# The float32 value products of the first attention batch: 64 columns of the array against 128

## The chip, the cores and the metric

The kernel runs on one core of a Trainium2 chip. The metric is the device time of one execution in microseconds (us); before the change it is 1199.45 us, the median of three runs from 1198.36 to 1200.13. Five engines work side by side, each through its own instructions in order: TensorE (PE, with its weight loads PEld), VectorE (DVE), ScalarE (ACT), GpSimd (POOL) and SyncE (SP), which here issues the DMA transfers.

## The reference

Four batches of eight heads, 576 positions, head width 64. In each head only the scores within `tau` of the row's largest one take part in the softmax. Behind the attention stand two feed-forward layers, all in float32:

```python
scores = scale * np.matmul(q, k.transpose(0, 1, 3, 2))
thresh = np.max(scores, axis=-1, keepdims=True) - tau
scores = np.where(scores >= thresh, scores, -1000000000.0)
scores = scores - np.max(scores, axis=-1, keepdims=True)
attn = np.exp(scores)
attn = attn / (np.sum(attn, axis=-1, keepdims=True) + 1e-09)
return np.matmul(attn, v).astype(np.float32)
...
return (silu * val @ w_out).astype(np.float32)      # width 512 -> 1536 -> 512
...
return (h * h @ w_out).astype(np.float32)           # width 512 -> 2048 -> 512
```

## The kernel before

**Tiles of attention.** Heads are handled in pairs, an even and an odd one; a batch has four pairs and a pair nine tiles of 128 rows of scores, so a batch is 36 tiles. For each tile TensorE forms the scores (`QK`, L575, 128x288 twice over), VectorE takes the row's maximum (`RED`, L587), ScalarE the exponential and the threshold (`EXP`, L593 and L595), VectorE masks and sums (`MASK`, L604) and takes the reciprocal (L610), GpSimd divides (`NORM`, L615), and TensorE transposes the tile in five 128x128 pieces (`TR`, L635). Scores have two buffers: the scores of a tile wait until the mask of the tile two before has been taken.

**The products with the values.** Four times in a pair (`AV`, parts 1, 4, 6, 8 of the nine tiles) five chunks of values are multiplied with the transposed tiles and summed in one PSUM bank. In the later batches this is done on numbers split into a rounded and a remaining part, with 128 columns of values (L694). In the first batch (`whole` is true there) it is done in float32 at once (L691): the five chunks lie beside each other in `vf`, 64 columns each, in a part of the tile `x2` that is not needed yet (`flat`). An even head's result goes to the lower 64 partitions of the bank and an odd head's to the upper 64 (`mr`); ScalarE copies that half to `xF`. The values come by DMA (`whole_values`, L452). The transposed tiles of the first batch lie in `ptf`, in the same `x2`, copied out by ScalarE and in one tile of nine in part by VectorE (L48, L50). One such product is in the program one instruction; on the engine it is two weight loads and two matmuls.

**Work around it.** A loader brings the weights of the first layer in 30 pieces of 256 columns: a DMA (L121), an absolute value on ScalarE (L130), four steps on VectorE (L132, L134, L138, L140), a rounding copy on ScalarE (L48) and a subtraction on GpSimd (L56). Its steps are spread over the tile loop by `loader.start` and `loader.tick`. From the end of the first batch on, feed-forward work on finished rows fills TensorE between the tiles (L219, L264); attention is over at about 460 us, and the rest is the two layers (L219, L264, L310).

**What sets the order.** The loop over tiles calls these functions in a fixed sequence with offsets of priority (`early0`, `early`), and a scheduler then orders each engine's instructions by priorities and its own costs. So another cost of one instruction can move others. The lines that matter here:

```python
c0 = 5 * 640 + h % 4 * VW
hd["vf"] = flat[:, c0 : c0 + VW].rearrange("p (c d) -> p c d", d=D)
...
mm(o[mr, :n], hd["vf"][:, SLOT[k], :], ptf[:, k, lo : lo + n], start=(k == 0), stop=(k == 4))
```

Of the kernel before, what the change touches and what calls it, by code (L numbers as in the profile page):

```python
# [18 lines left out]
P = 128  # L19
B, H, S, D = 4, 8, 576, 64  # L20
# [13 lines left out]
VW = 5 * D  # L34
# [28 lines left out]
def attention_moe(tc, qkv, qk0, tau, w1, w2, out, cfg):  # L63
    nc = tc.nc
    ops = Ops(nc)
    mm = nc.tensor.matmul
# [316 lines left out]
    for j in range(LIVE):  # L383
        c0 = LAST + j * PIECE
# [53 lines left out]
    flat = x2[0][1].rearrange("p c t -> p (c t)")  # L438
    ptf = flat[:, : 5 * 640].rearrange("p (s q) -> p s q", q=640)

    def whole(p, i):

        ways = cfg["way"][p // NPAIR % len(cfg["way"])]
        return p < NPAIR and ways[i] in "FEKD"

    def whole_values(h):
        hd = heads[h]
        if any(whole(h // 2, i) for i, x in PARTS.items() if x[2] == hd["odd"]):
            c0 = 5 * 640 + h % 4 * VW
            hd["vf"] = flat[:, c0 : c0 + VW].rearrange("p (c d) -> p c d", d=D)  # L450
            a = 2 * S + hd["odd"] * VW
            nc.sync.dma_start(flat[:, c0 : c0 + VW], qkv[h // 2, :, a : a + VW])  # L452

    def values(hd, h, raw):
        odd = hd["odd"]
        whole_values(h)
        if all(whole(h // 2, i) for i, x in PARTS.items() if x[2] == odd):
            return
        v = raw[:, 2 * S + odd * VW : 2 * S + (odd + 1) * VW].rearrange("p (c d) -> p c d", d=D)
        vs = hd["vs"] = qp.tile([P, 5, P], F32R, name=f"vs{h}", tag="vs", bufs=3)  # L460
        hi, lo = vs[:, :, odd * D : (odd + 1) * D], vs[:, :, (1 - odd) * D : (2 - odd) * D]
        ops.copy(cfg["vh"], hi, v)
        ops.sub(cfg["vl"], lo, v, hi.bitcast(F32))
# [84 lines left out]
    SLOT = (0, 1, 4, 2, 3)  # L548
# [132 lines left out]
    def AV(t):  # L681
        b, p, i = tiles[t]
        lo, n, odd, segs = PARTS[i]
        hd = heads[b * H + 2 * p + odd]
        no, o = mp1.tile()
        mr = slice(D, P) if odd else slice(0, D)
        cr = slice(0, D) if odd else slice(D, P)
        one = whole(b * NPAIR + p, i)
        if one:
            for k in range(5):  # L690
                mm(o[mr, :n], hd["vf"][:, SLOT[k], :], ptf[:, k, lo : lo + n], start=(k == 0), stop=(k == 4))  # L691
        else:
            for k in range(10):
                mm(o[:, :n], hd["vs"][:, SLOT[k % 5], :], pt[:, k, lo : lo + n], start=(k == 0), stop=(k == 9))  # L694
        base = b * S
        out_x = [(xF[mr, p, base + dst : base + dst + w], slice(src, src + w)) for dst, src, w in segs]

        def main():
            for x_, sl in out_x:
                ops.copy("A" if not one else cfg["om"], x_, o[mr, sl])  # L700
            if one:
                end()

        def fin():
            for x_, sl in out_x:
                nc.vector.tensor_tensor(x_, x_, o[cr, sl], op=ALU.add)
            end()

        def end():
            if i == 8 and p == NPAIR - 1:  # L710
                fstate["done"] = b

        if one:
            mp1.post(no, (cfg["om"], main))
        else:
            mp1.post(no, ("A", main), ("D", fin))
# [58 lines left out]
    def work(i):  # L775

        fstate["credit"] += cfg["rate"]
        if avq:
            at_(AV, avq.pop(0))
            if fstate["credit"] < cfg["extra"]:  # L780
                return
        if fstate["credit"] > 0:
            y = at_(fill_group)
            if y is None:
                fstate["credit"] = 0
            else:
                fstate["credit"] -= y
# [19 lines left out]
    for i in range(NTILE + lag + 1):  # L807
# [36 lines left out]
        if i < NTILE:  # L844
            b, p, k = tiles[i]
# [184 lines left out]
def program(arrays):  # L1030
    import concourse.bacc as bacc

    nc = bacc.Bacc("TRN2", target_bir_lowering=False, num_devices=1, dynamic_dma_scratch_size=1024)
    args = [nc.dram_tensor(n, a.shape, mybir.dt.from_np(a.dtype), kind="ExternalInput").ap() for n, a in arrays]
    out = nc.dram_tensor("out_0_dram", (NT, DM), F32, kind="ExternalOutput").ap()
    with tile.TileContext(nc) as tc:
        attention_moe(tc, *args, out, CFG)
    return nc
# [9 lines left out]
```

## Time and profile before

| what | value |
|---|---|
| median of three runs | 1199.45 us |
| the profiled execution, its own time | 1198.72 us |
| its span in the trace | 1196.9 us |
| PE / DVE / ACT / POOL busy over the span | 97% / 73% / 54% / 25% |
| first batch's products with the values (L691) | 160 matmuls, 20.3 to 117.5 us |

The times of the trace count from the start of the span; 1.8 us of the execution lie outside it. The shares over the whole span are a mean over stages that differ: attention alone to about 118 us, attention with feed-forward work between to about 460, and feed-forward layers after that. A busy PE is one on which a matmul is under way; matmuls overlap, so durations of single matmuls add up to more than the time they take, and the distance from one start to the next is what a matmul costs. "issue" is waiting for nothing that the profile shows.

### The profile page before, as it was taken

The numbers are of one execution on the slowest core, as the hardware profiler recorded it, in microseconds if no ns is written. First come the engines' busy times: TensorE is split into PE (matmuls) and PEld (weight loads), VectorE is DVE, ScalarE is ACT, GpSimd is POOL, SyncE is SP. The second block draws the span as 40 slices with busy tenths as digits, with TensorE's granted clock in tenths as the row PEclk, the third lists the DMA queues.
The fourth block names the chain that finished last, engine by engine and source line by source line (L and its number), as shares of the span: only waits on it lengthen the run. The fifth ranks groups of instructions, "written<-read, shape, count | busy, mean of one in ns | idle before, by whom it ended". The sixth has DMA issues, their size and how long they took to land.

```text
span 1196.9 us, 20191 instructions
## 1 busy us (share of the span) xinstructions
PE 1162.6 (97%) x7008; PEld 1074.8 (90%) x7008; DVE 868.2 (73%) x2143; ACT 652.1 (54%) x1622; POOL 293.8 (25%) x417
## 2 busy tenths in 40 slices
PE   5999998999999999999999999999999999999998
PEld 4555887999999999999999999999999899999997
DVE  6877997799989895789965954468449748754443
ACT  5777887888777774545432532145546425533221
POOL 4445875676776663000000000000000000000000
PEclk9999998999999999999999999999999999999999
DMA  5664452444334310332310300003002201100111
GB/s 177 151 182 127 127 134 66 109 116 110 94 97 106 93 36 1 108 104 80 98 36 7 108 29 1 1 18 104 21 1 80 62 1 54 36 1 1 53 54 53
DMA packets 40853, 84.79 MB, mean 71 GB/s; under 512 B 5936, under 2 KB 6960, under 8 KB 40752
## 3 DMA queue, kind: packets, MB, share of 16 engines
q1 hardware_dynamic: 40752, 83.52, 24.9%
q8 instruction: 55, 0.90, 0.3%
q14 instruction: 46, 0.38, 0.1%
HBM read 52.23 MB, written 4.72 MB: 48 GB/s over the span
## 4 chain that ended last, share of the span: by engine, by line
PE 79%; DVE 9%; DMA 3%; ACT 3%; issue 2%; POOL 2%; SPq 1%; POOLq 0%; DVEq 0%; ACTq 0%
PE mm L219 30%; PE mm L310 15%; PE mm L264 9%; PE s L575 5%; PE bank L635 5%; PE bank L219 4%; PE bank L264 4%; PE bank L694 4%; PE bank L691 3%; DMA wr<-in_w_dram 2%; DVE e L604 2%; DVE nm L587 1%; POOL e L615 1%; DMA raw<-in_qkv_dram 1%; DVE xs_k L56 1%
## 5 line engine op out<-in xcount | busy, mean ns | idle before, releaser
L219 PE MATMUL mm<-xs_k,w 128*128 128x384 f32 (+1 forms) x2400 | 413.2, 330 | 0.5 <-ACT x L48 0.5
L219 PEld LDWEIGHTS mm<-xs_k,w 128*128 128x128 f32 x2400 | 407.8, 188 | 2.5 <-ACT x L48 0.7
L310 PE MATMUL mm<-w,k_u 128*128 128x512 f32 x864 | 201.3, 391 | 0.3 <-DVE k_u L56 0.3
L310 PEld LDWEIGHTS mm<-w,k_u 128*128 128x128 f32 x864 | 161.5, 188 | 34.0 <-DVE k_u L56 1.0
L635 PE MATMUL bank<-ident,e 128*128 128x128 f32 x720 | 162.9, 278 | 6.4 <-POOL e L615 1.9
L219 PE MATMUL bank<-xs_m,w 128*128 128x288 f32 x720 | 137.1, 325 | 2.4 <-DVE xs_m L56 1.7
L615 POOL TENSOR_SCALAR e<-e,r 128x576 f32<-128x576 f32 x144 | 113.8, 791 | 83.6 <-DVE r L610 34.4
L604 DVE SCALAR_TENSOR_TENSOR e<-s,thr,e 128x577 f32<-128x577 f32 x144 | 117.0, 813 | 14.7 <-ACT thr L595 7.2
L48 ACT ACTIVATE k_u<-k_th 128x384 fp32r<-128x384 f32 (+1 forms) x148 | 76.3, 516 | 90.0 <-DVE k_th L294 47.0
L587 DVE TENSOR_REDUCE nm<-s 128x1 f32<-128x576 f32 x144 | 108.3, 753 | 17.7 <-PE s L575 16.6
L635 PEld LDWEIGHTS bank<-ident,e 128*128 128x128 f32 x720 | 95.2, 141 | 28.7 <-issue 15.9
L56 DVE TENSOR_TENSOR k_u<-k_th,k_u 128x384 fp32r<-128x384 f32 (+1 forms) x148 | 81.2, 549 | 47.8 <-ACT k_u L48 47.4
L219 PEld LDWEIGHTS bank<-xs_m,w 128*128 128x128 f32 x720 | 111.1, 189 | 5.1 <-DVE xs_m L56 3.4
L593 ACT ACTIVATE e<-s,nm 128x576 f32<-128x576 f32 x144 | 107.4, 746 | 14.3 <-PE bank L635 7.0
L655 ACT ACTIVATE pt<-bank 128x384 fp32r<-128x384 f32 (+1 forms) x216 | 92.1, 437 | 35.1 <-PE bank L635 28.9
L293 ACT ACTIVATE k_th<-mm 128x384 f32<-128x384 f32 x96 | 46.3, 483 | 111.0 <-PE mm L219 110.9
L264 PE MATMUL mm<-k_u,w 128*128 128x384 f32 (+1 forms) x624 | 106.1, 327 | 0.6 <-DVE k_u L56 0.4
L264 PEld LDWEIGHTS mm<-k_u,w 128*128 128x128 f32 x624 | 103.7, 188 | 1.0 <-DVE k_u L56 0.6
L694 PE MATMUL bank<-pt,vs 128*128 128x256 f32 (+1 forms) x480 | 93.5, 324 | 1.3 <-POOL pt L56 1.2
L575 PE MATMUL s<-kh,qs 128*128 128x288 f32 x256 | 78.1, 319 | 14.2 <-DVE qs L484 7.2
L294 DVE TENSOR_TENSOR k_th<-k_th 128x384 f32<-128x384 f32 x96 | 53.3, 555 | 52.4 <-ACT k_th L293 52.1
L48 ACT ACTIVATE w<-wf 128x256 fp32r<-128x256 f32 x116 | 46.8, 413 | 57.0 <-DVE wf L140 43.3
(90 smaller groups left out, 1697.0 us busy)
## 6 DMA issues: line engine op xcount, KB each, us to landing
wr<-in_w_dram SPq DMA_DIRECT2D x106, 256.0 KB, 3.0
raw<-in_qkv_dram SPq DMA_DIRECT2D x15, 896.0 KB, 4.7
kh<-land SPq DMA_DIRECT2D x60, 144.0 KB, 2.5
kl<-raw SPq DMA_DIRECT2D x60, 144.0 KB, 2.7
xF<-in_w_dram SPq DMA_DIRECT2D x30, 256.0 KB, 2.9
out_dram<-xF SPq DMA_DIRECT2D x18, 256.0 KB, 2.0
qs<-land SPq DMA_DIRECT2D x30, 144.0 KB, 2.4
qs<-raw SPq DMA_DIRECT2D x30, 144.0 KB, 2.6
```

The costliest lines, as they stand in the source:

```text
L48: nc.scalar.activation(out, in_, AF.Copy)
L56: e.tensor_tensor(out, a, b, op=ALU.subtract)
L219: mm(pt[:, :n], w[:, a, col + c * P : col + (c + 1) * P], xs[:, b, c, :], start=(i == 0), stop=(i == len(TERMS) - 1),)
L264: mm(pt[:, :n], w[:, a, 2 * DM + m * P : 2 * DM + (m + 1) * P], u[:, b, :], start=(k == 0), stop=(k == last),)
L310: mm(pt, u[:, b, s * P : (s + 1) * P], w[:, a, DM : 2 * DM], start=(k == 0), stop=(k == last),)
L575: mm(sp[:, cols], l, r[:, cols], start=(n_ == 0), stop=(n_ == len(pairs) - 1),)
L587: nc.vector.tensor_reduce(nm, sv, axis=AX.X, op=ALU.max, negate=True)
L593: nc.scalar.activation(e[:, :S], st[t]["s"][:, :S], AF.Exp, bias=st[t]["nm"])
L604: nc.vector.scalar_tensor_tensor(e, st[t]["s"][:, : S + 1], st[t]["thr"], e, op0=ALU.is_ge, op1=ALU.mult, accum_out=sum_)
L615: nc.gpsimd.tensor_scalar(e, e, scalar1=r, scalar2=1.0, op0=ALU.mult, op1=ALU.mult)
L635: mm(dst[:, j], e[:, c0 : c0 + P], ident, is_transpose=True, start=(j == 0), stop=(j == len(cols) - 1),)
L694: mm(o[:, :n], hd["vs"][:, SLOT[k % 5], :], pt[:, k, lo : lo + n], start=(k == 0), stop=(k == 9))
```

## The change

The values of a head get 384 columns instead of 320: an even head has its five chunks first and 64 zeros behind them, an odd head 64 zeros first and the chunks behind them. The zeros are written once by four GpSimd memsets (128x64). Each product then takes 128 neighbouring columns: the chunk that is wanted and, in the half that is not used, the next chunk (even head), the one before (odd head), or zeros. The result fills all 128 partitions of the bank; the half that is read is the same as before.

```diff
+    for h in range(4):
+        c0 = 5 * 640 + h * (VW + D) + (1 - h % 2) * VW
+        nc.gpsimd.memset(flat[:, c0 : c0 + D], 0.0)
...
-            c0 = 5 * 640 + h % 4 * VW
-            hd["vf"] = flat[:, c0 : c0 + VW].rearrange("p (c d) -> p c d", d=D)
+            c0 = 5 * 640 + h % 4 * (VW + D)
+            hd["vf"] = flat[:, c0 : c0 + VW + D]
+            c0 += hd["odd"] * D
...
-                mm(o[mr, :n], hd["vf"][:, SLOT[k], :], ptf[:, k, lo : lo + n], start=(k == 0), stop=(k == 4))
+                mm(o[:, :n], hd["vf"][:, SLOT[k] * D : SLOT[k] * D + P], ptf[:, k, lo : lo + n], start=(k == 0), stop=(k == 4))
```

Lines from 450 on stand six further down in the changed kernel, so L587 is L593 there, L604 is L610, L610 is L616, L635 is L641 and L691 is L697. The scheduler also orders the first 204 us or so differently. On TensorE, at the first product of the first batch (L691, `bank` from `x`, between transposes L635 of `e` and scores L575), before:

```order
L635 MATMUL bank_83<-ident,e_97 128x128 x2
L691 MATMUL bank_85<-x_65 64x256
L635 MATMUL bank_83<-ident,e_97 128x128
L635 MATMUL bank_84<-ident,e_97 128x128
L691 MATMUL bank_85<-x_65 64x256
L635 MATMUL bank_84<-ident,e_97 128x128
L691 MATMUL bank_85<-x_65 64x256 x3
```

and in the changed kernel:

```order
L641 MATMUL bank_83<-ident,e_97 128x128 x2
L697 MATMUL bank_85<-x_65 128x256
L641 MATMUL bank_83<-ident,e_97 128x128
L697 MATMUL bank_85<-x_65 128x256
L641 MATMUL bank_84<-ident,e_97 128x128
L697 MATMUL bank_85<-x_65 128x256
L641 MATMUL bank_84<-ident,e_97 128x128
L697 MATMUL bank_85<-x_65 128x256 x2
```

The product writes 128 partitions instead of 64, and one transpose moved between the second and third of the five.

On VectorE, in the first batch, from the 21st to the 23rd maximum (`nm` from `s`; `e` are masks, `r` reciprocals, `xF` and `wf` loader steps), before:

```order
L610 RECIPROCAL r_708<-sum_707 128x1
L587 TENSOR_REDUCE nm_748<-s_108 128x1
L56 TENSOR_TENSOR xs_m_1340<-xF,xs_m_1340 128x288
L604 SCALAR_TENSOR_TENSOR e_97,sum_743<-s_107,thr_714,e_97 128x577
L604 SCALAR_TENSOR_TENSOR e_95,sum_771<-s_108,thr_749,e_95 128x577
L610 RECIPROCAL r_744<-sum_743 128x1
L610 RECIPROCAL r_772<-sum_771 128x1
L587 TENSOR_REDUCE nm_777<-s_107 128x1
```

and in the changed kernel:

```order
L132 TENSOR_SCALAR wf_78<-wf_78 128x256
L134 TENSOR_SCALAR wf_78<-wf_78 128x256
L593 TENSOR_REDUCE nm_752<-s_108 128x1
L610 SCALAR_TENSOR_TENSOR e_97,sum_747<-s_107,thr_718,e_97 128x577
L138 SCALAR_TENSOR_TENSOR wf_78<-xF,wf_78 128x256
L616 RECIPROCAL r_748<-sum_747 128x1
L132 TENSOR_SCALAR xF<-xF 128x256
L140 SCALAR_TENSOR_TENSOR wf_78<-xF,wf_78 128x256
L610 SCALAR_TENSOR_TENSOR e_95,sum_775<-s_108,thr_753,e_95 128x577
L533 SCALAR_TENSOR_TENSOR raw_743<-raw_743,qscale,land_745 128x576
L616 RECIPROCAL r_776<-sum_775 128x1
L593 TENSOR_REDUCE nm_781<-s_107 128x1
```

Five loader steps now stand between the same maxima, where there were none.

Later on VectorE, in the second batch, from the 56th to the 57th maximum (`pt` splits a transposed tile, `xF` from `bank` adds a product's second half; the other `xF` and `wf` are loader steps), before:

```order
L587 TENSOR_REDUCE nm_2157<-s_108 128x1
L134 TENSOR_SCALAR xF<-xF 128x256
L610 RECIPROCAL r_2151<-sum_2150 128x1
L132 TENSOR_SCALAR xF<-xF 128x256
L138 SCALAR_TENSOR_TENSOR xF<-xF 128x256
L134 TENSOR_SCALAR xF<-xF 128x256
L140 SCALAR_TENSOR_TENSOR xF<-xF 128x256
L138 SCALAR_TENSOR_TENSOR xF<-xF 128x256
L706 TENSOR_TENSOR xF<-xF,bank_84 64x64
L140 SCALAR_TENSOR_TENSOR xF<-xF 128x256
L604 SCALAR_TENSOR_TENSOR e_96,sum_2247<-s_108,thr_2158,e_96 128x577
L587 TENSOR_REDUCE nm_2254<-s_107 128x1
```

and in the changed kernel:

```order
L593 TENSOR_REDUCE nm_2161<-s_108 128x1
L610 SCALAR_TENSOR_TENSOR e_95,sum_2154<-s_107,thr_2109,e_95 128x577
L616 RECIPROCAL r_2155<-sum_2154 128x1
L610 SCALAR_TENSOR_TENSOR e_96,sum_2251<-s_108,thr_2162,e_96 128x577
L593 TENSOR_REDUCE nm_2258<-s_107 128x1
```

The seven loader steps that stood there have all moved ahead.

## Rows read from the trace of the kernel before

**Rows 1.** Stretches: length; PE, PEld, DVE, ACT, POOL busy (count); clock, DMA share, GB/s.

```profile
20.00:118.00 98.00, 93.56 (x477) 56.21 (x476) 79.36 (x199) 71.84 (x187) 47.55 (x67) 1.00 0.57 152
118.00:144.00 26.00, 24.81 (x182) 23.46 (x182) 24.84 (x61) 23.57 (x65) 20.86 (x28) 1.00 0.42 103
...
118.00:204.00 86.00, 76.56 (x520) 70.09 (x520) 78.94 (x190) 69.19 (x185) 61.58 (x80) 0.96 0.43 113
```

**Rows 2.** Chain of waits, 20 to 118 us, shares by line.

```profile
by line: PE bank L691 37.6%; PE bank L635 18.6%; PE s L575 16.9%; issue 10.4%; POOL e L615 4.9%; POOL raw L56 2.3%; ACT x L48 1.7%; POOL w L56 1.5%; ACT e L593 1.4%; POOL vs L52 1.0%; DVE e L604 0.8%; DVE nm L587 0.8%; ACT xF L48 0.8%; POOL
```

**Rows 3.** Waits of VectorE, 20 to 118 us: total us, times, longest.

```profile
DVE nm L587 <- PE s L575: 8.3, 14, 1.2
```

**Rows 4.** Chain of waits, 140 to 206 us: start, length, work.

```profile
149.88 1.00 DVE xF L138
...
189.05 1.62 POOL w L56 x2
```

**Rows 5.** Chain of waits, whole span: two runs of L691.

```profile
22.18 1.44 PE bank L691 x6
...
115.62 2.32 PE bank L691 x10
```

**Rows 6.** Timeline of PE: start, length, form, count.

```profile
20.33 0.65 PE L691 MATMUL bank<-x 128*64 128x256 f32 x2
20.91 0.44 PE L635 MATMUL bank<-ident,e 128*128 128x128 f32 x2
21.28 0.65 PE L691 MATMUL bank<-x 128*64 128x256 f32 x2
...
37.52 0.29 PE L575 MATMUL s<-kl,qs 128*128 128x288 f32 x1
37.65 0.38 PE L635 MATMUL bank<-ident,e 128*128 128x128 f32 x2
37.79 0.38 PE L575 MATMUL s<-kh,qs 128*128 128x288 f32 x1
38.00 0.30 PE L575 MATMUL s<-kl,qs 128*128 128x288 f32 x1
...
115.55 2.37 PE L691 MATMUL bank<-x 128*64 128x256 f32 x10
```

**Rows 7.** Weight loads by form, 20 to 118 us: busy us, mean ns.

```profile
L691 PEld LDWEIGHTS bank<-x 128*64 128x64 f32 x160 | 17.9, 135 | 13.8 <-issue 3.9 <-ACT x L48 1.1
L575 PEld LDWEIGHTS s<-kh,qs 128*128 128x128 f32 x60 | 11.4, 190 | 6.8 <-DVE e L604 2.8 <-DVE r L610 1.3 <-DVE xF L140 1.0
```

**Rows 8.** Loader steps by line, 20 to 118 us: busy us, mean ns.

```profile
L140 DVE SCALAR_TENSOR_TENSOR xF<-xF 128x256 int32<-128x256 int32 x9 | 3.9, 433 | 0.0
L138 DVE SCALAR_TENSOR_TENSOR xF<-xF 128x256 int32<-128x256 int32 x8 | 3.7, 472 | 0.0
L134 DVE TENSOR_SCALAR xF<-xF 128x256 int32<-128x256 int32 x8 | 3.4, 439 | 0.0
L132 DVE TENSOR_SCALAR xF<-xF 128x256 f32<-128x256 f32 x9 | 3.4, 375 | 0.2 <-ACT xF L130 0.2
...
L48 ACT ACTIVATE w<-xF 128x256 fp32r<-128x256 f32 x9 | 3.6, 415 | 0.0
...
L56 POOL TENSOR_TENSOR w<-xF,w 128x256 fp32r<-128x256 f32 x9 | 6.8, 754 | 10.9 <-ACT w L48 10.9
```

**Rows 9.** Timeline from 0 us, GpSimd at the start.

```profile
1.45 0.50 POOL L414 MEMSET qt<- 128x128 f32 x3
...
4.88 0.67 POOL L52 TENSOR_SCALAR kh<-raw 128x576 fp32r<-128x576 f32 x1 [2.93 <-DMA raw<-in_qk_dram]
```

**Rows 10.** Stretches where the granted clock changed (columns as in rows 1).

```profile
177.00:183.60 6.60, 4.39 (x28) 3.45 (x27) 6.54 (x14) 5.02 (x15) 4.79 (x6) 1.00 0.40 110
183.60:187.00 3.40, 3.24 (x16) 2.84 (x15) 3.34 (x11) 2.47 (x8) 1.20 (x2) 0.50 0.25 58
...
190.40:193.80 3.40, 3.08 (x13) 3.09 (x14) 1.36 (x5) 1.97 (x6) 1.75 (x3) 0.50 0.02 5
```

## The prediction, made before the changed kernel ran

> **What bounds the kernel now.** I read the busy time by stretch first, because only the first batch of attention heads contains the products that change. Between 20 and 118 us TensorE (PE) is busy 93.56 of 98 us, VectorE (DVE) 79.36, ScalarE (ACT) 71.84, GpSimd (POOL) 47.55 [rows 1]. The reader should see one engine nearly full and a second at 81%. The chain of waits of that stretch says the same: 37.6% of it is the changed line (L691), 18.6% the transposes, 16.9% the scores, and 10.4% is "issue", time in which the engine waited for nothing that the profile shows [rows 2]. VectorE's largest wait there is for the scores of TensorE, 8.3 us in 14 waits [rows 3]. So in this stretch TensorE sets the pace. From 118 to 204 us it is no longer alone: VectorE is busy 78.94 of 86 us, TensorE 76.56 [rows 1], and the chain goes for long pieces through VectorE's and GpSimd's steps of the weight loader [rows 4]. After 204 us the program's order is the same in both kernels on every engine; nothing there changes by itself.
>
> **Where TensorE's time in the first batch goes.** A float32 product is two hardware instructions, so the 80 products of L691 are 160 matmuls. A chain piece of 6 takes 1.44 us and one of 10 takes 2.32 us [rows 5], so each further matmul of 256 columns costs 0.88 / 4 = 0.22 us. Now look at a short run in the timeline: two matmuls of L691 begin at 20.33 and the transposes behind them at 20.91, 0.58 us for work worth 0.44; the two transposes then last until 21.28, 0.37 us [rows 6]. Transposes between two scores show the price without a break: from the score at 37.52 to the score at 38.00 there are two scores and two transposes in 0.48 us [rows 6], and a run of scores has one each 0.13, so the two transposes cost 0.22. Hence a run of L691 loses 0.14 us going in (a stop, then a first load that is not hidden) and 0.15 coming out. The timeline has 48 such runs from 20.33 to 115.55 (first and last in [rows 6]), so 48 x 0.295 = 14.2 us of TensorE's 93.56 is change-over. Scores and transposes, 128 columns wide both, show none among themselves. The only thing that sets L691 apart in width is its 64 columns.
>
> **The change, part by part.**
>
> *128 columns in L691.* The instruction count stays. The columns that stream through stay (256 or 320), so the 0.22 us stays. The weight load grows: 135 ns with 64 columns, 190 with 128 [rows 7], 55 ns more. Inside a run it starts a whole matmul ahead (0.22 us) and is hidden as the loads of the scores are behind their 0.13 us; I take 0 there. If the cover were gone it would be 160 x 0.055 = 8.8 us. The change-overs go: 14.2 us off TensorE, which leaves 79.4.
>
> *The order.* The scheduler now puts the loader's steps earlier. Counting VectorE's loader steps (four to each piece of 256 columns, L132 to L140) ahead of the 36th maximum, the last of the first batch, gives 49 before and 70 now; by the 60th maximum both have all 120. So 21 steps move from the second stretch to the first. The four kinds last 375, 439, 472 and 433 ns [rows 8], mean 0.43: 9.0 us. With them come 6 absolute-value and 6 rounding copies on ScalarE (some 0.42 us each by the row of the second [rows 8], 5 us) and 5 subtractions on GpSimd (754 ns [rows 8], 3.8 us); both engines have that room.
>
> *The four memsets.* They stand on GpSimd ahead of the first head's rounding copy. GpSimd waits 2.93 us for that copy's DMA, and three memsets of twice the width take 0.50 us [rows 9]. Cost 0, hidden by that wait; without the wait at most 0.7 us. The value loads change address only.
>
> *First stretch, 20 to 118.* TensorE falls to 79.4, ScalarE rises to 77, VectorE rises to 79.36 + 9.0 = 88.4: VectorE becomes the bound. How full can it be? From 118 to 144 us all four engines were loaded and VectorE was busy 24.84 of 26 us, 95.5%, TensorE 24.81 [rows 1]. I take that: 88.4 / 0.955 = 92.6 us, **5.4 us** less. The ends: VectorE full to the brim gives 88.4 (9.6 less); VectorE at its present 81% gives 109 (11 more).
>
> *Second stretch, 118 to 204.* VectorE falls to 78.94 - 9.0 = 69.9 and TensorE's 76.56 becomes the bound. At the 95.4% of the same row it needs 76.56 / 0.954 = 80.3 us, **5.7 us** less. One end is 0, if the waits on loads and on GpSimd hold it. The other: in two pieces of 3.4 us TensorE ran at half clock (granted 0.50, that is 1.2 GHz) and was busy 3.24 and 3.08 us [rows 10]; at 2.4 GHz that work takes 3.2 us less, 73.4 / 0.954 = 76.9, 9.1 us less. I stay near the middle.
>
> *The rest.* Same order, TensorE full: 0, give or take 1 us.
>
> Sum against the profiled execution's own 1198.72 us: 1198.72 - 5.4 - 5.7 = 1187.6. That execution lies 0.73 under the median of 1199.45, so on the median's footing 1188.3.
>
> **The rivals.**
>
> *The stop belongs to float32, not to the width.* No row shows a float32 product 128 columns wide, so the stretch cannot part the two. Then the change-overs stay, and each of the 48 entries loads 128 columns in the open, 48 x 0.055 = 2.6 us more; VectorE at 88.4 of 100 us still fits. The second stretch still gains 5.7: 1199.4 + 2.6 - 5.7 = 1196.3, and about 1200 if the second stretch gives only half. For it: transposes are float32 too, but of another mode. Against: the two halves of a float32 product follow each other without a stop. The Trainium skill, "TensorEngine Tiling (Array Packing)", Key Properties, says that changing the tiling mode, and not just the tile, drains the engine; by that rule the whole 14.2 us goes. I give this rival 0.11.
>
> *The wider loads are not hidden.* For it: the first load of each run is in the open now [rows 6]. Against: loads of 190 ns already lie behind matmuls shorter than these. TensorE would keep 8.8 of the 14.2 us, have 88.2 us of work beside VectorE's 88.4, and with two engines equally full the first stretch would give perhaps 3: 1199.4 - 3 - 5.7 = 1190.7. The Trainium skill, "TensorE: Matmul & The Clock Gate", LDWEIGHTS, counts a load by its columns alone, over 1.2 GHz: 53 ns more here, an estimate of 8.5 us for 160 loads, which speaks against the change; the rows give the same growth but not that it shows. Chance 0.03.
>
> *The loader's steps now stand in front of the maxima and masks* (the slower side). VectorE works in order; a step of 0.43 us ahead of a maximum delays the exponential, the mask, and with it the score buffer that TensorE needs. If VectorE cannot get past its present 81% with this order, the first stretch takes 109 us, 11 more, and the second gives 5.7 back: 1199.4 + 11 - 5.7 = 1204.7. It decides at 88.4 / (98 + 5.7) = 85% of VectorE: below that, slower. Against: 95.5% right behind, with the same kinds of instructions [rows 1]. Chance 0.07.
>
> *The clock falls in the first batch.* TensorE would be busy 79.4 of 92.6 us, 86%, where now it is 95%. In 177 to 183.6 it was busy 4.39 of 6.6 us, and the clock was then granted at 0.50 for 3.4 us [rows 10]. Three such pieces at the first batch's idle spots, each at most 1.7 us of TensorE work, cost 5: 1193.4. Chance 0.06.
>
> *More than forecast.* VectorE at 99% in the first stretch (89.3 us, 8.7 less) and the half clock gone in the second (9.1 less): 1181.6. Chance 0.13.
>
> **How the numbers follow.** The forecast itself, 1184 to 1193, has 0.60. What can be told from no change is about 0.2%, 2.4 us, so 1197.0 to 1201.9 counts as the same. Faster: 0.60 + 0.13 + 0.06 + 0.03 and a bit under half of 0.11, with something held back for causes I do not see: 0.85. Same: the rest of the float32 rival and weak outcomes, 0.08. Slower: 0.07. The range for 8 in 10 goes from 1180, just under the larger gain, to 1197, the float32 rival's 1196.3 included.
>
> **What would show it.** In the changed kernel: runs of L691's line with no "issue" idle ahead of the weight load behind them; L691's loads near 190 ns and the spacing inside runs still 0.22; a chain over the first batch in which that line's share falls and VectorE's rises; first batch over by 113 us; TensorE near 86% and VectorE near 95% in it. In the second stretch, fewer loader pieces on the chain and the point of 204 us reached near 193. The prediction is wrong at its first step if transposes still start late behind L691, at its second if VectorE stays under 90% in the first batch, and at its third if the second stretch keeps its 86 us although its VectorE work fell by 9.

## The result and the profile after

The changed kernel takes **1188.02 us** (median of six runs, 1186.42 to 1190.47) against 1199.05 for the kernel before in the same runs (1198.07 to 1202.77): a ratio of 0.9906, 95% interval 0.9888 to 0.9925, 11.0 us less. The profiled execution of the changed kernel took 1190.41 us, its span is 1187.6; the one of before had 1198.72 and 1196.9. TensorE is busy 1149.6 us in it, 1162.6 before, 13.0 us less; VectorE, ScalarE and GpSimd are busy within 1.4 us of what they were.

**The change-overs are gone.** The timeline of TensorE in the changed kernel shows the first product run; columns are start, length, then engine, line and form (start to start is the price):

```profile
20.84 0.44 PE L641 MATMUL bank<-ident,e 128*128 128x128 f32 x2 [0.55 <-POOL e L621]
21.11 0.60 PE L697 MATMUL bank<-x 128*128 128x256 f32 x2
21.55 0.27 PE L641 MATMUL bank<-ident,e 128*128 128x128 f32 x1
21.66 0.60 PE L697 MATMUL bank<-x 128*128 128x256 f32 x2
22.09 0.27 PE L641 MATMUL bank<-ident,e 128*128 128x128 f32 x1
22.20 0.60 PE L697 MATMUL bank<-x 128*128 128x256 f32 x2
```

Two products and a transpose take 0.55 us (21.11 to 21.66): twice 0.22 and once 0.11, with nothing in between. In [rows 6] two products and two transposes took 0.95 (20.33 to 21.28) where 0.66 was work. The weight loads of the changed kernel, grouped by line from 20 to 118 us (busy us, mean ns, idle time of the load queue before them and what ended it), tell the same:

```profile
L697 PEld LDWEIGHTS bank<-x 128*128 128x128 f32 x160 | 27.0, 195 | 10.1 <-ACT x L48 4.2 <-issue 0.2
L641 PEld LDWEIGHTS bank<-ident,e 128*128 128x128 f32 x175 | 21.7, 141 | 10.0 <-POOL e L621 5.2 <-POOL vs L52 1.0 <-POOL w L56 0.6
```

Against [rows 7] the loads grew from 135 to 195 ns and the 3.9 us of "issue" ahead of them became 0.2. For the transposes the same view of the kernel before had this line:

```profile
L635 PEld LDWEIGHTS bank<-ident,e 128*128 128x128 f32 x172 | 20.2, 140 | 20.8 <-issue 14.1 <-POOL e L615 3.9 <-ACT x L48 1.6
```

Its 14.1 us of "issue" have left the list. So the wider loads cost nothing that shows, and of some 18 us of waiting for nothing 0.2 us is left.

**The first batch ended hardly earlier.** Stretches of the changed kernel, columns as in [rows 1]:

```profile
20.00:118.00 98.00, 86.06 (x489) 69.36 (x488) 91.20 (x230) 80.05 (x207) 56.91 (x78) 0.98 0.62 168
118.00:144.00 26.00, 23.10 (x164) 21.20 (x164) 25.80 (x59) 20.90 (x58) 18.73 (x25) 1.00 0.54 137
118.00:204.00 86.00, 80.54 (x589) 76.18 (x589) 76.36 (x179) 70.56 (x188) 58.01 (x79) 1.00 0.42 106
```

VectorE now does 91.20 us of work in the first stretch, 11.8 more than in [rows 1]. That is the loader: its four kinds of step, grouped by line over the same stretch of the changed kernel (those on `xF`; the `wf` ones make another 26):

```profile
L138 DVE SCALAR_TENSOR_TENSOR xF<-xF 128x256 int32<-128x256 int32 x13 | 6.2, 486 | 0.0
L140 DVE SCALAR_TENSOR_TENSOR xF<-xF 128x256 int32<-128x256 int32 x13 | 5.8, 445 | 0.0
L132 DVE TENSOR_SCALAR xF<-xF 128x256 f32<-128x256 f32 x14 | 5.3, 385 | 0.5 <-ACT xF L130 0.5
...
L134 DVE TENSOR_SCALAR xF<-xF 128x256 int32<-128x256 int32 x13 | 5.2, 413 | 0.1
```

53 of them where [rows 8] had 34; with `wf` 79 where there were 52. They stand on the chain too. Shares of the chain from 20 to 118 us in the changed kernel, and three of its longest pieces (start, length):

```profile
by line: issue 16.7%; DVE e L610 13.6%; DVE nm L593 10.6%; DMA raw<-in_qkv_dram 7.5%; PE bank L697 6.0%; PE s L581 3.9%; DVE xF L138 3.7%; SPq L522 3.7%; PE bank L641 3.1%; DMA kl<-raw 2.9%; DVE wf L140 2.8%; DVE r L616 2.5%; DVE xF L132 2.
...
55.20 1.51 SPq L522
58.04 2.81 DMA kl<-raw
60.92 7.38 DMA raw<-in_qkv_dram
```

The products fell from 37.6% [rows 2] to 6.0%, masks and maxima rose to 24%. And VectorE hardly waits for the scores any more; its longest waits are now for the exponential (waits of VectorE, 20 to 118 us: total, times, longest; [rows 3] had 8.3 us for the scores):

```profile
DVE e L610 <- ACT e L599: 2.4, 2, 1.3
...
DVE nm L593 <- PE s L581: 1.0, 4, 0.4
```

**Where the time came back.** I laid the two traces side by side by progress, not by clock. Counted along VectorE's timeline, the next maximum begins, after so many tiles, at (us):

| tiles done | 36 | 54 | 60 | 66 | 72 |
|---|---|---|---|---|---|
| before | 109.1 | 173.5 | 200.9 | 219.9 | 239.2 |
| after | 107.9 | 173.4 | 193.2 | 209.5 | 228.8 |

At the end of the first batch the changed kernel is 1.2 us ahead, after 54 tiles 0.1, after 60 tiles 7.7 and after 66 tiles 10.4; at the end of the spans 9.3 are left. The last product of the first batch begins at 117.2 us instead of 117.5. The stretch up to tile 36, first before, then after:

```profile
20.00:109.10 89.10, 84.72 (x435) 51.17 (x434) 74.06 (x185) 67.28 (x174) 44.77 (x63) 1.00 0.56 147
```

```profile
20.00:107.90 87.90, 76.62 (x439) 62.15 (x437) 81.87 (x206) 71.21 (x184) 50.50 (x70) 0.98 0.61 163
```

TensorE has 8.1 us less to do there, VectorE 7.8 us more, in 21 more instructions: nearly a swap. From tile 36 to tile 54 the changed kernel loses 1.1 us again, and there VectorE is full: 64.17 of 65.50 us, 98%, against 58.60 of 64.40 before (before, then after):

```profile
109.10:173.50 64.40, 59.97 (x409) 52.36 (x408) 58.60 (x142) 51.89 (x141) 45.85 (x61) 1.00 0.49 131
```

```profile
107.90:173.40 65.50, 59.94 (x411) 53.85 (x410) 64.17 (x150) 54.37 (x144) 47.68 (x64) 1.00 0.50 131
```

The stretch from tile 54 to tile 60, before and after:

```profile
173.50:200.90 27.40, 22.33 (x134) 19.68 (x132) 24.84 (x64) 21.14 (x56) 16.53 (x21) 0.88 0.34 97
```

```profile
173.40:193.20 19.80, 19.25 (x147) 18.75 (x147) 13.31 (x36) 16.06 (x43) 11.17 (x16) 1.00 0.33 90
```

Here the loader steps are missing that have been done earlier: VectorE had 24.84 us of work in 27.40 and has 13.31 in 19.80. TensorE, at half clock for two pieces of that stretch [rows 10], is now busy 19.25 of 19.80 at full clock.

### The profile page after: what moved, and what is told of

It is laid out like the page before. It is cut to its first block, busy times and chain, and to the rows that moved or that the text cites. A ratio compares the mean times of both kernels' runs of the same rounds, so it can differ in the third digit from the quotient of the medians.

```text
span 1187.6 us, 20194 instructions
## 1 busy us (share of the span) xinstructions
PE 1149.6 (97%) x7008; PEld 1083.4 (91%) x7008; DVE 869.6 (73%) x2143; ACT 653.3 (55%) x1622; POOL 294.4 (25%) x421
## 4 chain that ended last, share of the span: by engine, by line
PE 69%; DVE 16%; DMA 5%; issue 4%; ACT 4%; POOL 1%; SPq 1%; POOLq 0%; DVEq 0%; ACTq 0%
PE mm L219 28%; PE mm L310 13%; PE mm L264 8%; PE bank L219 4%; PE bank L264 4%; PE s L581 4%; PE bank L700 3%; PE bank L641 3%; DMA wr<-in_w_dram 3%; DVE e L610 3%; DVE nm L593 2%; DMA raw<-in_qkv_dram 1%; DVE wf L138 1%; DVE wf L140 1%; DVE xs_k L56 1%
## 5 line engine op out<-in xcount | busy, mean ns | idle before, releaser
L641 PE MATMUL bank<-ident,e 128*128 128x128 f32 x720 | 163.0, 275 | 7.5 <-ACT x L48 3.6
L610 DVE SCALAR_TENSOR_TENSOR e<-s,thr,e 128x577 f32<-128x577 f32 x144 | 116.8, 813 | 14.6 <-ACT e L599 11.0
L593 DVE TENSOR_REDUCE nm<-s 128x1 f32<-128x576 f32 x144 | 108.0, 751 | 6.9 <-PE s L581 6.0
L641 PEld LDWEIGHTS bank<-ident,e 128*128 128x128 f32 x720 | 96.9, 141 | 16.4 <-POOL e L621 5.7
L581 PE MATMUL s<-kh,qs 128*128 128x288 f32 x256 | 80.5, 328 | 16.0 <-DVE e L610 8.4
```

The lines of the kernel that those rows point to most:

```text
L581: mm(sp[:, cols], l, r[:, cols], start=(n_ == 0), stop=(n_ == len(pairs) - 1),)
L593: nc.vector.tensor_reduce(nm, sv, axis=AX.X, op=ALU.max, negate=True)
L610: nc.vector.scalar_tensor_tensor(e, st[t]["s"][:, : S + 1], st[t]["thr"], e, op0=ALU.is_ge, op1=ALU.mult, accum_out=sum_)
L641: mm(dst[:, j], e[:, c0 : c0 + P], ident, is_transpose=True, start=(j == 0), stop=(j == len(cols) - 1),)
```

## The experiments

All times are medians, with the ratio to the kernel before, run beside them. "Steps" are VectorE's loader steps ahead of the 36th maximum: 49 before, 70 after.

**Is it the width or the order?** Four runs: the change with its loader held back, and the kernel before with another order or another layout.

*w128_held*: the changed kernel; a loader piece's DMA also waits for the reciprocal of two tiles ago, so the loader can't run ahead.

```diff
+            if self.gate is not None:
+                ops.copy("P", raw.bitcast(F32)[:, 0:1], self.gate)
             nc.sync.dma_start(raw, src[f, :, sl])
...
+        loader.gate = st[i - 2].get("r") if 2 <= i < NTILE + 2 else None
...
```

> The changed kernel (128 columns) with the weight loader held back: before each piece's DMA, GpSimd copies one column of the reciprocals of the tile two before into the piece's buffer, so the piece cannot start earlier. Counted in the program's order, 50 loader steps of VectorE stand ahead of the 36th maximum (49 in the kernel before, 70 in the changed one). Theory A (the change-overs of TensorE are gone, and from there VectorE's work up to 204 us sets the time, wherever its loader steps stand): the first batch ends some 10 us earlier than before, near 107 us, the second stretch keeps its 86 us, the time is about 1188 (1186 to 1192). Theory B (the gain is the scheduler's new order, loader steps moved out of the crowded second stretch; the width gives nothing by itself): 1199 (1197 to 1201). Theory C (the width alone, order without effect): 1188, as A, with products and transposes without stops.

Measured: 1194.85 us, 0.9964 (0.9951 to 0.9976), 50 steps. Faster than before with before's count of steps, but not 1188: it lies in the range of none of the three theories. The hold may have a price of its own, so this run alone doesn't part them; ScalarE now waits for the weights' DMA (its waits, 20 to 108 us):

```profile
ACT xF L133 <- DMA xF<-in_w_dram: 6.3, 5, 1.6
```

*w64_early*: the kernel before, with priorities that let the loader go first in the first batch.

```diff
-        "AV": -2, "PS": 16, "NORM": 34, "EXP": 32, "LA": 20, "FP": -100, "PL": 30, "fill_group": -40,
-        "RED": -12, "RCP": 4, "MASK": 4, "NEG": -60,
+        "AV": -2, "PS": 16, "NORM": 34, "EXP": 32, "LA": 200, "FP": -100, "PL": 30, "fill_group": -40,
+        "RED": -12, "LD": 200, "RCP": 4, "MASK": 4, "NEG": -60,
```

> The kernel before (64 columns) with the loader's steps raised in priority in the first batch: 69 of VectorE's 120 steps stand ahead of the 36th maximum, as in the changed kernel (70), and 20 instead of 5 ahead of the 6th. The products stand in 54 runs instead of 48. Theory A: TensorE stays full in the first batch (6 runs more, 6 x 0.295 = 1.8 us) and gets VectorE's extra steps beside it, so the first batch is 2 to 4 us longer, the second stretch some 6 shorter: about 1196 (1193 to 1200). Theory B: 1188. Theory C: 1199 to 1201.

Measured: 1202.76 us, 1.0030 (1.0019 to 1.0040), 69 steps. With about the changed kernel's count of steps and 64 columns it is 3.8 us slower than before, not faster. All three theories missed it, but the order alone does not bring the gain. Tile 36 is reached at 120.2 us, 11 later than before.

*w64_pad*: the changed kernel's layout of values, memsets and addresses, but products of 64 columns.

```diff
-                mm(o[:, :n], hd["vf"][:, SLOT[k] * D : SLOT[k] * D + P], ptf[:, k, lo : lo + n], start=(k == 0), stop=(k == 4))
+                mm(o[mr, :n], hd["vf"][:, (SLOT[k] + odd) * D : (SLOT[k] + odd + 1) * D], ptf[:, k, lo : lo + n], start=(k == 0), stop=(k == 4))
```

> The changed kernel's layout of the values and its four memsets, but each product takes the 64 columns of its own chunk and writes 64 partitions, as before. 53 runs of products, 55 loader steps ahead of the 36th maximum. Theory A: 53 - 48 = 5 runs more (1.5 us), a little of the loader moved ahead: 1199 (1196 to 1201). Theory B: about a quarter of the move of order, 1196. Theory C: 1199 to 1201. If the layout or the memsets were what pays, 1188.

Measured: 1199.54 us, 1.0002 (0.9992 to 1.0012), 55 steps. Layout and memsets are worth nothing that shows.

*w64_together*: the kernel before, with the products of a block kept together, so that 48 runs become 26.

```diff
-        "AV": -2, "PS": 16, ...
+        "AV": 60, "PS": 16, ...
```

> The kernel before (64 columns) with the products raised in priority in the first batch, so that the five of one sum mostly follow each other: 26 runs instead of 48. 68 loader steps stand ahead of the 36th maximum. Theory A: TensorE saves 22 x 0.295 = 6.5 us of change-overs, about half of what the wide products save, and the order is the early one: about 1192 (1190 to 1195). Theory B: 1188. Theory C, where only the runs count: 1199 - 11 x 22 / 48 = 1194.

Measured: 1207.81 us, 1.0078 (1.0062 to 1.0093). 22 change-overs fewer, worth 6.5 us at 0.295 each, and yet slower by 8.8, which none of the theories had. "Issue" ahead of the transposes' loads did fall, from 14.1 to 4.5 us, but blocks of ten float32 matmuls (2.3 us) now stand in front of the scores, and VectorE waits for these 12.1 us where it was 8.3 (20 to 118 us):

```profile
DVE nm L587 <- PE s L575: 12.1, 7, 2.8
```

So fewer change-overs don't help where the order of the rest suffers. The run says nothing for or against their price.

**The width at one placement.** The first four leave open what the hold itself costs.

*w64_held*: the same hold in the kernel before (the diff of w128_held).

> The kernel before (64 columns) with the same hold on the weight loader as in w128_held: GpSimd copies a column of the reciprocals of the tile two before into a piece's buffer ahead of its DMA. 49 loader steps ahead of the 36th maximum (50 in w128_held), 52 runs of products. The pair tells the width's worth at one placement of the loader, free of what the hold itself costs. Theory D (the change-overs are worth most of their 14 us wherever TensorE sets the pace, and the hold costs several us in both): 1203 (1200 to 1207), that is 6 to 12 above w128_held's 1194.9. Theory E (at a late placement the width is worth only the 4 us by which w128_held beat the kernel before, and the hold costs nothing): 1199 (1197 to 1201).

Measured: 1207.52 us, 1.0067 (1.0047 to 1.0086), half a us over the range of 1200 to 1207. The hold costs 7.7 us at 64 columns, and the pair with and without width, at the same hold, differs by 1207.52 - 1194.85 = **12.7 us** (12.4 by the two ratios). The granted clock is no part of that: over the runs it is 0.996 and 0.995 in the mean. The two traces are further apart than the medians, 17.7 us of span, as that of w64_held was taken in the slowest of its six executions (1211.90 us). In them tile 36 is reached at 119.8 against 107.5 us, so 12.3 of the 17.7 lie in the first batch. The stretches up to there, w64_held and then w128_held:

```profile
20.00:119.80 99.80, 90.86 (x440) 53.55 (x439) 74.19 (x186) 68.18 (x175) 48.82 (x78) 0.97 0.52 139
```

```profile
20.00:107.50 87.50, 77.25 (x436) 62.99 (x435) 75.19 (x189) 67.87 (x177) 48.46 (x78) 0.96 0.57 153
```

VectorE's work is the same within 1.0 us, TensorE's is 13.6 less, and the time is 12.3 less. The clock is nearly the same too, 0.97 and 0.96. This is the cleanest view of the change: with as many loader steps ahead of the 36th maximum (49 and 50), time of the size of the change-overs comes off the first batch. w64_held has 52 runs of products, at 0.295 us 15.3 us.

*w64_mid*: the kernel before with a milder shift of the loader (one entry of the table: `"LD": 110`).

> The kernel before (64 columns) with a smaller raise of the loader's VectorE steps than in w64_early: 6 steps ahead of the 6th maximum (5 before, 5 in the changed kernel), 62 ahead of the 36th (49 and 70). 54 runs of products. Asked: what the changed kernel's order is worth while TensorE still has its change-overs. Theory D (TensorE sets the first batch's pace with them, so the steps moved ahead ride along for free at best, and the second stretch gains little): 1200 (1198 to 1203). Theory B (the order alone): 13 of the 21 steps moved, 13 / 21 of 11 us: 1192.

Measured: 1200.55 us, 1.0008 (0.9999 to 1.0016), 62 steps; tile 36 at 117.9 us. At 64 columns 13 more steps make the first batch 8.8 us longer (there are also 54 runs of products instead of 48, 1.8 us of it), and all of it comes back later. The order alone, as far as this run has it, is worth nothing: the 1200 that was expected by one theory, not the 1192 of the other.

**What limits the changed kernel?** If VectorE, then work taken off it must help, and work added must cost.

*w128_pmax*: the changed kernel; in the first phase the loader's maximum (L132) runs on GpSimd.

```diff
-            yield "D"
-            nc.vector.tensor_scalar(fl, fl, scalar1=F64_MIN, scalar2=None, op0=ALU.max)
+            yield "DP"[self.phase == 0]
+            (nc.vector if self.phase else nc.gpsimd).tensor_scalar(fl, fl, scalar1=F64_MIN, scalar2=1.0, op0=ALU.max, op1=ALU.mult)
```

> The changed kernel with one of the loader's four VectorE steps (L132, the maximum with a constant) done by GpSimd during attention. 30 steps of 0.38 to 0.43 us leave VectorE, some 12 us up to 194 us; GpSimd gets 30 steps of about 0.75 us, 22 us. Theory D (with the change-overs gone, VectorE is what sets the time up to 194 us): 1183 (1180 to 1186). Theory F (no engine is the bound by its sum; waits from engine to engine in the tile loop are, and GpSimd's divisions now wait behind the new steps): 1188 to 1192.

Measured: 1202.51 us, 1.0029 (1.0018 to 1.0039), 14.5 slower than the changed kernel: both theories missed. The step takes a mean of 1.10 us on GpSimd against 0.385 on VectorE. GpSimd's groups by line, then the stretch, 20 to 118 us:

```profile
L132 POOL TENSOR_SCALAR xF<-xF 128x256 f32<-128x256 f32 x12 | 13.1, 1096 | 2.8 <-ACT xF L130 2.8
...
L132 POOL TENSOR_SCALAR wf<-wf 128x256 f32<-128x256 f32 x6 | 6.6, 1093 | 2.4 <-ACT wf L130 2.4
```

```profile
20.00:118.00 98.00, 81.50 (x448) 65.08 (x447) 81.13 (x200) 72.60 (x190) 71.56 (x90) 0.95 0.58 152
```

VectorE, TensorE and ScalarE all do less than in the changed kernel, and GpSimd 14.7 us more. VectorE's next step of the loader (L134) now waits for GpSimd's, 7.1 us in all, and TensorE's waits for masks (in the two buffers of scores) come to 8.3 us, where the changed kernel had 4.0 in the same stretch:

```profile
DVE xF L134 <- POOL xF L132: 4.9, 7, 1.1
...
DVE wf L134 <- POOL wf L132: 2.2, 3, 1.7
```

```profile
PE s L581 <- DVE e L610: 8.3, 9, 2.7
```

The step became nearly three times as long and stands in the middle of a chain that VectorE then waits for, so the run says nothing on VectorE as the bound. How much of the 14.5 us goes to this and how much to GpSimd's divisions, which share the engine, was not parted.

*w128_together*: the changed kernel with the products of a block together (as w64_together; 20 runs).

> The changed kernel with the products raised in priority as in w64_together: 20 runs of products instead of 52, 103 loader steps ahead of the 36th maximum. There are no change-overs to save here. Theory D: nothing on TensorE is gained, scores wait behind blocks of ten matmuls (2.2 to 2.7 us) and VectorE for them: 1193 to 1199. Theory C (only the number of runs and their price count): 1188, as the changed kernel.

Measured: 1200.34 us, 1.0003 (0.9990 to 1.0016), a little over 1193 to 1199, and far from 1188. Grouping costs some 12 us here against 8.8 at 64 columns. That there are no change-overs left to save fits this; but the loader moved as well (103 steps, and tile 36 only at 125.4 us), so neither price is that of grouping alone.

*w128_dmax* and *w64_dmax*: each kernel with the loader's maximum done twice for each piece of the first layer, 30 more steps of VectorE, some 11 us by the 0.375 of [rows 8].

```diff
-            nc.vector.tensor_scalar(fl, fl, scalar1=F64_MIN, scalar2=None, op0=ALU.max)
+            for _ in range(1 if self.phase else 2):
+                nc.vector.tensor_scalar(fl, fl, scalar1=F64_MIN, scalar2=None, op0=ALU.max)
```

> The changed kernel with one VectorE step of the loader (L132, the maximum with a constant, which gives the same again) done twice for each of the 30 pieces of the first layer: 30 x 0.4 = 12 us more work on VectorE up to about 194 us, nothing else. Theory D (with the change-overs gone VectorE sets the time there): 9 to 12 us more, 1198 (1196 to 1201). Theory F (waits from engine to engine set it, VectorE's sum does not): at most 4 more, 1188 to 1192.

Measured: 1195.27 us, 0.9961 (0.9947 to 0.9974), 7.3 over the changed kernel (6.6 by the two ratios): between the two theories. By progress, none of the loss lies in the first batch. The scheduler put 73 steps, doubles included, ahead of the 36th maximum, where the changed kernel has 70, so the first batch has only three more; tile 36 is reached at 105.2 us and tile 54 at 171.7, both earlier than in the changed kernel (107.9 and 173.4). Tile 60 then comes at 200.0 instead of 193.2. The stretch from tile 54 to tile 60 of w128_dmax:

```profile
171.70:200.00 28.30, 23.78 (x153) 22.23 (x151) 22.88 (x56) 19.14 (x51) 15.88 (x20) 0.88 0.29 83
```

It looks like that of the kernel before (27.40 us, clock 0.88), with the loader steps that were left over.

> The same doubled step in the kernel before (64 columns). Theory D: in the first batch TensorE sets the pace and covers the extra steps, in the second stretch VectorE does; 60 of now 150 steps stand ahead of the 36th maximum, so about 18 of the 30 doublings fall behind it: 18 x 0.43 = 7.7 us more, 1206 (1203 to 1209), less than in w128_dmax. Theory F: at most 4 more, 1199 to 1203.

Measured: 1207.09 us, 1.0060 (1.0047 to 1.0073), 6.7 over the kernel before beside it, inside the range of theory D, and in size hardly less than the 7.3 of w128_dmax. So the added work costs about the same in both kernels, some 0.6 us for each us, but not all of that need be VectorE's time: the granted clock of TensorE is lower too, 0.996 and 0.995 in the mean of the runs of w128_dmax and w64_dmax against 0.999 in the changed kernel's and 0.998 in those of before. Three or four thousandths of 1200 us are, as an estimate, up to some 4 us of TensorE's work. The pair leaves open what limits the changed kernel; the one place where a row shows VectorE full is tile 36 to tile 54.

*w128_ways*: the changed kernel with one way code of the first batch's nine tiles changed, which takes the copies of transposed tiles (L50) off VectorE.

```diff
-    "way": ("FFKFFFFFF", "TTTIHTHTI", "IVHIIHVHV", "VVIVHIVIV"),
+    "way": ("FFFFFFFFF", "TTTIHTHTI", "IVHIIHVHV", "VVIVHIVIV"),
```

> The changed kernel with the one copy of transposed tiles in each pair of the first batch that VectorE made given to ScalarE: four copies of 0.55 us leave VectorE, and about as much comes to ScalarE (busy 80 of 98 us in the first stretch). 78 loader steps ahead of the 36th maximum. Theory D: 2.2 us less on the bound, at most 2 us faster than the changed kernel: 1186 (1185 to 1189). Theory F: 1188 or a little more, as ScalarE's copies then stand ahead of exponentials.

Measured: 1186.83 us, 0.9886 (0.9872 to 0.9901), 78 steps, tile 36 at 107.4 us. It is the lowest time of a kernel that does the whole work, 1.2 us under the changed kernel (2.4 by the ratios), but the intervals of the two ratios overlap.

**What makes the stop?** *w64_f32r*: the changed kernel; in the later batches the products of even heads (rounded numbers, a float32 form called fp32r) are 64 columns wide instead of 128. The part with the remainder of the values is left out in all heads of these batches, so its 1182.74 us (one run) is no time for this work; what counts is the sequence on TensorE.

```diff
-                mm(o[:, :n], hd["vs"][:, SLOT[k % 5], :], pt[:, k, lo : lo + n], start=(k == 0), stop=(k == 9))
+                c = slice(0, P) if odd else mr
+                mm(o[c, :n], hd["vs"][:, SLOT[k % 5], c], pt[:, k, lo : lo + n], start=(k == 0), stop=(k == 9))
...
```

> The changed kernel, but in the later three batches the products of the even heads take only the 64 columns of the rounded values and write 64 partitions; those of the odd heads stay 128 wide; in both the part with the remainder of the values is left out of the result. These are float32r products of one matmul each. If the stop belongs to the width: entering and leaving the 64-column runs costs 0.09 us each beside an open load, as in the float32 products of the kernel before, and the 128-column runs of the odd heads cost none. If it belonged to float32 products: neither shows a stop. The time itself is no part of the question; some 2 us for each 20 runs on TensorE.

Measured, TensorE's timeline in that kernel (L701 are the products):

```profile
133.13 0.29 PE L581 MATMUL s<-kl,qs 128*128 128x288 f32 x1
133.26 0.46 PE L701 MATMUL bank<-pt,vs 128*64 128x320 f32 x2
133.61 0.30 PE L641 MATMUL bank<-ident,e 128*128 128x128 f32 x1
133.67 0.39 PE L701 MATMUL bank<-pt,vs 128*64 128x320 f32 x1
133.90 0.27 PE L641 MATMUL bank<-ident,e 128*128 128x128 f32 x1
133.93 0.39 PE L701 MATMUL bank<-pt,vs 128*64 128x320 f32 x1
134.16 0.27 PE L641 MATMUL bank<-ident,e 128*128 128x128 f32 x1
134.18 0.39 PE L701 MATMUL bank<-pt,vs 128*64 128x320 f32 x1
```

One product and one transpose, in and out of 64 columns, take 0.25 to 0.26 us (133.67 to 133.93 to 134.18). With a transpose at 0.11 that leaves 0.14 to 0.15 for a product of 320 columns; a change-over of 0.295 has no room in it. From the score (133.13) to the first product it is 0.13, a score's usual distance. The odd heads of the same kernel, 128 columns wide, take the same 0.26 us for a product and a transpose:

```profile
173.45 0.39 PE L701 MATMUL bank<-pt,vs 128*128 128x320 f32 x1
173.68 0.27 PE L641 MATMUL bank<-ident,e 128*128 128x128 f32 x1
173.71 0.39 PE L701 MATMUL bank<-pt,vs 128*128 128x320 f32 x1
173.94 0.27 PE L641 MATMUL bank<-ident,e 128*128 128x128 f32 x1
173.97 0.39 PE L701 MATMUL bank<-pt,vs 128*128 128x320 f32 x1
```

So **64 columns alone don't stop the engine**. Nor does float32 alone (L697 above). Only the two together did, in the kernel before.

## Why the prediction came out right, and where it was off

**The sum held.** 1188.3 was forecast and 1188.02 measured; on the profiled spans 9.3 us went where 11.1 had been reckoned, and the medians differ by 11.0. That the sum is met to 0.3 us is luck: the changed kernel's runs spread over 4 us, and two terms are off by some 4 us each, one up and one down.

**Step one, TensorE's change-overs: right.** 14.2 us off TensorE were forecast. The page of the profile shows 13.0 less over the span, and the held pair 13.6 up to tile 36, with 12.3 us of time there. (In the changed kernel itself it is 8.1 up to tile 36, where 3.4 us of TensorE's time ran at half clock.)

**Step two, hidden loads: right.** 195 ns a load, and matmuls at the same 0.22 us spacing. The Trainium skill, "TensorE: Matmul & The Clock Gate", LDWEIGHTS, counts a load by its columns over 1.2 GHz, 53 ns more here; the measured growth of 60 ns is near that, though the transposes' loads, 128 columns too, take only 141 ns. The growth doesn't show in the spacing, so the 8.5 us estimated from the page's figure are not there.

**Step three, the order: right in kind, and up to tile 36 in size.** 21 steps and 9.0 us were forecast, 21 instructions and 7.8 us measured. But the stretch that the sum used ends at 118 us, about the 39th tile, and there the move is 27 steps and 11.8 us.

**Step four, the first stretch: mis-sized.** 5.4 us were forecast, 1.2 came by tile 36 and 0.1 by tile 54; the mark of the first batch over by 113 us was missed by 4, its last product beginning at 117.2. Two terms of it failed: VectorE had 91.20 us of work up to 118 us, not 88.4, and it was 93% busy, not 95.5% (91.20 of 98; up to tile 36 it is 81.87 of 87.90, also 93%). With 95.5% the 81.87 us would have taken 85.7, 2.2 us less than they did. TensorE is at 88%, near the 86 that was set as a mark. The occupancy had been borrowed from the stretch of 118 to 144 us. In the first batch three pieces of the chain shown above, 11.7 us between 55 and 68 us, run through the transfers of new heads and their issue; then TensorE is busy 1.95 of 4.5 us, and behind that it runs at half clock for 3.4 us (granted 0.50, 1.2 GHz), busy without a gap. The two stretches, columns as in [rows 1]:

```profile
72.50:75.90 3.40, 3.40 (x12) 2.74 (x11) 2.29 (x7) 2.20 (x7) 2.25 (x4) 0.50 0.70 154
...
68.00:72.50 4.50, 1.95 (x13) 1.52 (x13) 3.37 (x7) 4.12 (x10) 2.17 (x3) 1.00 0.62 151
```

That is the rival of the falling clock in small: one such piece, at most 1.7 us of TensorE's work, where the rival had three.

**Step five, the second stretch: mis-sized the other way.** 5.7 us were forecast, with 9.1 as the end if the half clock went. From tile 36 to tile 66 the changed kernel gained 9.2 us, and both pieces of half clock of [rows 10] are gone. The mark that was set, 204 us reached near 193, was 60 tiles reached at 193.2 instead of 200.9, some 195 to 196 for that point.

The two errors are linked: a loader step taken early costs in the first batch and is paid back behind it, as w64_mid shows at 64 columns, where 8.8 us lost up to tile 36 had all come back at the end. For that reason the sum is safer than its parts. Not all of it is shown to be one time: up to 3.2 us of the second gain is the half clock that went, which the prediction had as an end and not as its middle. What the prediction lacked is the account by progress instead of by clock.

**Rivals.** Float32 without regard to width (1196.3) falls with the first timeline above. Wider loads in the open (1190.7) fall by the spacing; the time alone, with runs up to 1190.47, would not have ruled them out. More than forecast (1181.6) did not come: the half clock went, but the first stretch gave next to nothing. The loader's steps in front of maxima and masks (1204.7) did not decide, as VectorE was at 93% and the point was 85%; yet with 64 columns these steps do cost: 13 more make the first batch 8.8 us longer (w64_mid) and 20 more 11.1 (w64_early), while the changed kernel took 21 more at 1.2 us less. That is the place where the freed time of TensorE went: as an estimate, 12.3 us of the held pair less the 11.1 of w64_early leaves about the 1.2 that were seen. The rule of the Trainium skill, "TensorEngine Tiling (Array Packing)", Key Properties, that a change of tiling mode drains the engine, gives the right time here. The products of w64_f32r go between 64 and 128 columns without a stop; whether rounded products 64 columns wide change the mode at all no run here shows, so they neither confirm the rule nor speak against it.

**What stays open.** Why float32 and 64 columns have to come together for the stop, and what else than VectorE between tile 36 and tile 54 limits the changed kernel. Rounded products 64 columns wide in the upper half were not tried. Nor was the changed kernel's exact order run with 64 columns; w64_early and w64_mid come near its counts only. And the changed kernel's own runs spread over 4 us (1186.42 to 1190.47), so differences of 1 or 2 us, that of w128_ways among them, are not settled.

## What to carry to other kernels

Price a change of mode by the distance from start to start of the instructions around it, not by their durations: 0.295 us for each run of products was in no instruction's length, and 48 of them were 14 us. When an edit frees time on one engine, look at what the order puts into it, and compare two traces at the same progress of the work; the gain may appear a hundred microseconds behind the place of the edit. To know what an edit is worth by itself, run it with and without at an order held as nearly fixed as can be, even if the hold costs something, since both sides pay it.

## What the runs showed of the hardware that was not expected

- TensorE stopped at the edges of runs of float32 products 64 columns wide (0.14 us in, 0.15 out, [rows 6]), not at those of float32 products 128 wide (0.22 and 0.11 us without a gap), and not at those of rounded products 64 wide (0.25 us for a product and a transpose).
- A 128x128 float32 load of 195 ns is hidden behind a matmul of the same full array that takes 0.22 us from start to start, and one of 190 ns behind scores that follow each other every 0.13.
- A maximum with a second operation on 128x256 float32 takes GpSimd 1.10 us in the mean (w128_pmax); the maximum alone takes VectorE 0.385 in the changed kernel, in the same stretch.
